# A routed two-layer network behind a sliding filter: a smaller first chunk, and three banks for the second product

## The chip, the cores and the metric

The kernel runs on one core of one Trainium2 chip. The metric is the device time of one execution in microseconds (us); lower is better. The engines are called as the profile calls them: PE (TensorE) multiplies matrices, DVE (VectorE) and ACT (ScalarE) work on elements, POOL (GpSimd) here mostly issues indirect DMAs (DMAs whose rows are picked by a list of indices), SP (SyncE) issues the plain ones.

## The reference

`x` is 8 x 3584 x 192 in float32. It is filtered along the sequence with 7 softmaxed taps for each of 8 heads of 24 columns; then each of the 28672 rows goes to one of 8 experts, the one with the largest logit, and through that expert's two layers:

```python
w = softmax(weight, axis=-1)                                 # 8 heads, 7 taps
out = np.einsum('hk,bskhg->bshg', w, windows_of(x_padded))   # causal filter
x = out.reshape(28672, 192)
logits = x @ w_gate + modality_bias[modality_id]             # 8 experts
e_idx, gate_w = argmax(logits), softmax(logits)[argmax]
for e in range(8):
    h = np.maximum(x[e_idx == e] @ w1[e], 0)                 # 192 -> 1024
    out[e_idx == e] = gate_w * (h @ w2[e])                   # 1024 -> 192
```

## The kernel before

**Routing by groups.** The rows are cut in 256 tiles of 112; four tiles are a quad, and `QUADS_OF_GROUP` makes 19 groups g0 to g18 of 1, 1, 2, 2, 2 and then 14 times 4 quads. A group is loaded (`x` or `xr`), filtered with one step for each head (`convolve`, PE tile `cv`, copied to `y` by ACT or DVE), turned and multiplied with the gate's weights (`turn`, `part_turned`, `gate`, `logits`: tiles `turned`, `gx`, `gt`, `lt`, `lg`), given its experts (`choose`) and its places among the rows of these (`place`: PE tile `rp`, then `idx`). At last one indirect DMA of POOL for each tile writes its 112 rows to the place in DRAM (`send`, tensor `routed_rows`, line 212); one such DMA is called a scatter here. There are four buffers `y`: a group of 4 quads takes two, and a filter step can only write one when its earlier scatters have landed. The first `WHOLE_X` groups are filtered with one product in full float32; for the later ones DVE and ACT split x into a high and a low part (`xh`, `xl`) and PE makes three faster products. `WHOLE_Y` does the same for the gate's product (`gx` are the split parts).

**The network by slots and passes.** The groups are bundled in chunks (`GROUPS_OF_CHUNK`), each with a fixed number of slots (`SLOTS_OF_CHUNK`), each of a fixed number of passes (`PASSES_OF_SLOT`) of 256 rows. A slot serves one expert with rows that are there: a small table (`table`, DVE, about 25 operations on one partition) picks expert and first row; SP reads it and loads the slot's weights (`raw`) and rows (`rows`, `ends`). ACT and DVE split the weights in two parts (`w1b`, `w2b`, line 100 and 101), PE turns the rows of a pass (`tp`), ACT and DVE split them (`sxh`, `sxl`, `sxs`), and the pass then has four steps (`fp` 0 to 3): ten matmuls of the first layer into `hps` (line 695), `hh` by ACT, `hl` by DVE, and, two steps later (`LAG`), eight matmuls of the second layer into `po` (lines 713 and 717). After the last one `put` makes `lowp` (ACT) and `o` (DVE) for both halves, and POOL writes them to the output with two indirect DMAs (line 732), the puts. Rows that fill no slot wait for a later chunk; the last chunk has slots of one pass, of which 8 always run.

**The order.** `start(0)` emits all of the first chunk's groups, the loads of slot 0, and then `AHEAD` more parts of the routing; this is called the head here. Then `run` emits step after step. Between steps it emits parts of the routing as fast as `due` says: `marks` lists the step by which the groups of a chunk must be routed, `LEAD` steps before the chunk begins. Step numbers count from 0 at the first `hps`; the first chunk has 32 steps, and 456 steps run in all. `TURN` is the step of a pass after which the next pass is turned. ACT keeps the order as written; on the other engines a scheduler may move instructions. PSUM has 8 banks: 2 for `hps`, 2 for `po`, 4 for everything else (`ps_t`: `tp`, `cv`, `gt`, `rp`).

Of the kernel before, what the change touches and what calls it, by code (L numbers as in the profile page):

```python
# [9 lines left out]
F32 = mybir.dt.float32  # L10
# [6 lines left out]
PSUM = bass.MemoryType.PSUM  # L17

P = 128
MB = 112  # L20
HALO = 16
QUADS_OF_GROUP = (1, 1, 2, 2, 2) + (4,) * 14
WHOLE_X = 10
WHOLE_Y = 5
HEAD_BANKS = dict(turn=1, logit=2, place=2)
ORDERED = {mybir.EngineType.Activation}
WARM = 50
# [1 line left out]
WAIT = 3  # L29
OUTS = 4  # L30
PIN = 18
AHEAD = 26
T = 256
GROUPS_OF_CHUNK = (5, 2, 2, 2, 2, 2, 2, 2, 0, 0)
SLOTS_OF_CHUNK = (4, 3, 3, 4, 3, 4, 3, 3, 3)
PASSES_OF_SLOT = (2, 4, 4, 4, 4, 4, 4, 4, 2, 1)
LEAD = 11
TURN = 1
LAG = 2
SURE = 8  # L40

# [2 lines left out]
def conv_then_routed_ffn(ctx, tc, x, weight, modality, w_gate, mod_bias, w1, w2, out):  # L44
# [30 lines left out]
    sp = ctx.enter_context(tc.tile_pool(name="sp", bufs=4))  # L75
    hp = ctx.enter_context(tc.tile_pool(name="hp", bufs=4))
    ps_g1 = ctx.enter_context(tc.tile_pool(name="ps_g1", bufs=2, space=PSUM))
    ps_g2 = ctx.enter_context(tc.tile_pool(name="ps_g2", bufs=2, space=PSUM))
    ps_t = ctx.enter_context(tc.tile_pool(name="ps_t", bufs=4, space=PSUM))

    halves = slice(0, DB), slice(DB, P)
    turns = {}
# [1 line left out]
    def ring(pool, n, shape, dtype, name, tag=None):  # L84

        tag = tag or name
        k = turns[tag] = turns.get(tag, -1) + 1
        return pool.tile(shape, dtype, name=name, tag=f"{tag}_{k % n}", bufs=1)
# [94 lines left out]
    def make_modality():  # L183
        both = const.tile([MB, 2, E], F32, name="both")
        nc.scalar.dma_start(out=both.rearrange("p m e -> p (m e)"),
                            in_=mod_bias.rearrange("m e -> (m e)").partition_broadcast(MB))
        step = const.tile([MB, E], F32, name="step")
        nc.vector.tensor_tensor(out=step, in0=both[:, 1, :], in1=both[:, 0, :], op=ALU.subtract)
        rows = N // MB
        ids = raw2[1].rearrange("p c d -> p (c d)")[:, 0:2 * MB * rows // P].bitcast(I32).rearrange("p (q s) -> p q s", s=2 * MB)  # L190
        nc.scalar.dma_start(out=ids, in_=modality.bitcast(I32).rearrange("(q p s) -> p q s", p=P, s=2 * MB))
        low = raw2[1].rearrange("p c d -> p (c d)")[:, 2 * MB * rows // P:3 * MB * rows // P].rearrange("p (q s) -> p q s", s=MB)
        nc.vector.tensor_copy(out=low, in_=ids.rearrange("p q (s two) -> p q s two", two=2)[:, :, ::-1, 0])
        mt_ps = ring(ps_t, 4, [MB, rows], F32, "mt_ps", "t")
        for q in range(rows // P):
            nc.tensor.transpose(out=mt_ps[:, q * P:(q + 1) * P], in_=low[:, q, :], identity=ident)
        mt = const.tile([MB, NB, NSB], F32, name="mt")
        nc.vector.tensor_copy(out=mt.rearrange("p b s -> p (b s)"), in_=mt_ps)
        return both[:, 0, :], step, mt
# [24 lines left out]
    class Group:  # L224
# [13 lines left out]
        def bank(self, use, *args):  # L238

            if self.chunk > 0 or use not in HEAD_BANKS:  # L240
                return ring(ps_t, 4, *args, "t")
            if HEAD_BANKS[use] == 1:
                return ring(ps_g1, 2, *args, "hps")
            return ring(ps_g2, 2, *args, "po")

        def load(self, q):

# [18 lines left out]
        def convolve(self, h):  # L266
            if h == 0:
                self.ys = [routed_y() for _ in range(self.blocks)]
            cv = ring(ps_t, 4, [MB, self.tiles, G], F32, "cv", "t")
            hs = slice(h * G, (h + 1) * G)  # L270
            if self.whole_x:
                terms = ((band, self.x[:, 0:self.tiles, :]),)
            else:
                terms = (band_hi, self.xh), (band_hi, self.xl), (band_lo, self.xh)
            for n, (wt, xt) in enumerate(terms):
                nc.tensor.matmul(cv, wt[:, h, :], xt[:, :, hs], start=n == 0, stop=n == len(terms) - 1)  # L276
            ys = slice(2 + h * G, 2 + (h + 1) * G)
            for i, y in enumerate(self.ys):
                src = cv[:, i * self.nb:(i + 1) * self.nb, :]
                if h % 3 < 2:  # L280
                    nc.scalar.copy(out=y[0:MB, 0:self.nb, ys], in_=src)  # L281
                else:
                    nc.vector.tensor_copy(out=y[0:MB, 0:self.nb, ys], in_=src)
# [165 lines left out]
    def all_groups():  # L449

        cur, ends = Group(0, 0), iter(())
        for q in range(cur.quads):
            cur.load(q)
            cur.part(q)
        for g in range(NG):
            after = Group(g + 1, chunk_of[g + 1]) if g + 1 < NG else None
            done, tiles = 0, 4 * QUADS_OF_GROUP[g - 1]
            for i, _ in enumerate(body(cur, after)):
                yield
                if g < FIRST:  # L460
                    if 1 <= i < H:
                        next(ends, None)
                        if i == H - 1:
                            for _ in ends:
                                pass
                else:
                    while done * (parts_of(g) - 4) < (tiles + 1) * i:
                        next(ends, None)
                        done += 1
            for _ in ends:  # L470
                pass
            ends = finish(cur, 4 if g < FIRST else 1)
            if g + 1 in (FIRST, NG):
                for _ in range(WAIT):
                    yield
                for _ in ends:
                    yield
            cur = after
# [129 lines left out]
    class Slot:  # L608
# [55 lines left out]
        def turn(self, k):  # L664
            lot, k0 = divmod(k, LOT)
            rows = self.rows[lot][:, k0 * NJ:(k0 + 1) * NJ, :]
            tp = ring(ps_t, 4, [P, NJ + 1, P], F32, "tp", "t")
            for j in range(NJ):
                nc.tensor.transpose(out=tp[:, j, :], in_=rows[:, j, 2:2 + P], identity=ident)  # L669
            nc.tensor.transpose(out=tp[:, NJ, :], in_=self.ends[lot][:, k0].rearrange("p j d -> p (j d)"), identity=ident)  # L670
            xh = ring(sp, 2, [P, NJ, P], F32R, "sxh")
            xl = ring(sp, 2, [P, NJ, P], F32R, "sxl")
            xs = ring(sp, 2, [P, NJ, P], F32R, "sxs")
            pieces = [(xh, xl, tp[:, 0:NJ, :])]
            pieces += [(xs[halves[j], j, :], xs[halves[1 - j], j, :], tp[halves[j], NJ, :]) for j in range(NJ)]
            for hi, _, raw in pieces:
                nc.scalar.copy(out=hi, in_=raw)  # L677
            for hi, lo, raw in pieces:
                turned = nc.vector.tensor_tensor(out=lo, in0=raw, in1=f(hi), op=ALU.subtract).ins  # L679
            tag = ring(sp, 8, [P, NJ, 2], F32, "tag")  # L680
            with tc.issue_after(turned):
                nc.vector.tensor_copy(out=tag, in_=rows[:, :, 0:2])
            self.h["x", k] = [z.rearrange("p j s -> p (j s)") for z in (xh, xl, xs)]
            self.h["tag", k] = tag
            state["vector"] = turned
# [16 lines left out]
        def second(self, k, fp):  # L702
            wb = w2b[self.i % 2]
            hh, hl = self.h.pop((k, fp))
            if fp == 0:
                self.po = [ring(ps_g2, 2, [P, 2 * D], F32, "po") for _ in range(NJ)]
            for u in range(2):
                c = 2 * fp + u
                for j, po in enumerate(self.po):
                    js = slice(j * P, (j + 1) * P)  # L710

                    def by_hi():
                        nc.tensor.matmul(po, hh[:, u, js], wb[:, c, :], start=c == 0, stop=c == NF - 1,  # L713
                                         skip_group_check=True)

                    def by_lo():
                        nc.tensor.matmul(po[:, 0:D], hl[:, u, js], wb[:, c, 0:D], start=False, stop=False,  # L717
                                         skip_group_check=True)

                    for product in (by_lo, by_hi) if c == NF - 1 else (by_hi, by_lo):  # L720
                        product()
            if fp == NF // 2 - 1:
                self.put(self.h.pop(("tag", k)))
# [54 lines left out]
    for c in range(1, last):  # L778
        steps += plan[c - 1][1] * steps_of(c - 1)
        g = sum(GROUPS_OF_CHUNK[:c + 1])  # L780
        if not GROUPS_OF_CHUNK[c]:
            break
        marks.append((steps - LEAD, head + sum(parts_of(i) for i in range(FIRST, min(g + 1, NG)))
                      + (WAIT + 2 + 4 * QUADS_OF_GROUP[-1] if g == NG else 0)))

    def due(step):
        for (s0, p0), (s1, p1) in zip(marks, marks[1:]):
# [137 lines left out]
```

## Time and profile before

| | us |
|---|---|
| runs of the kernel before: median (lowest to highest of 3) | 1295.89 (1295.55 to 1296.23) |
| the profiled execution, and its span | 1294.9, 1293.2 |
| PE busy in the span | 1247.0 |
| DVE, ACT, POOL busy in the span | 982.2, 701.5, 523.2 |
| mean granted clock of PE | 0.985 of full speed |

The page gives busy times of one profiled execution, the one line of 40 slices for each engine, and the groups of instructions. A busy PE in it is not PE at its peak, since matmuls overlap; the price of a stretch of PE work is read from the starts of its instructions. Numbers like "75.63" are microseconds from the start of the span.

### The profile page before, as it was taken

The page shows a single profiled execution, that of the slowest core. Times are in us where ns is not written, and L with a number is a line of the kernel's source. Part 1 is how long each engine was busy: PE and PEld are TensorE (multiplying, and loading weights), DVE is VectorE, ACT ScalarE, POOL GpSimd, SP SyncE. Part 2 cuts the span into 40 slices and gives each one's busy share as a digit, 9 for nine tenths or more (in the row PEclk, how much of TensorE's full clock was granted, in tenths as well). Part 3 has the DMA queues.
Part 4 walks back from the last instruction along what each step waited for, and adds up shares of the span by engine and source line. Part 5 has one row for each costly group of instructions (what it writes and reads, how often), then busy time and mean ns, then how long its engine had stood idle before and what let it go on. Part 6 is the DMA issues. An engine that isn't in the chain of part 4 may idle for free.

```text
span 1293.2 us, 27020 instructions
## 1 busy us (share of the span) xinstructions
PE 1247.0 (96%) x9448; PEld 1219.8 (94%) x9448; DVE 982.2 (76%) x2431; ACT 701.5 (54%) x1644; POOL 523.2 (40%) x574
## 2 busy tenths in 40 slices
PE   8559999999999999999999999999999999999997
PEld 7348899999999999999999999999999999999996
DVE  6569977887888677877888777877776666577895
ACT  2236664565656556555555555555554454455784
POOL 5736762626262622625354442614426122122121
PEclk9779999999999999999999999999999999999999
DMA  6576462523443224413254334413314123683230
GB/s 177 158 207 185 122 183 55 144 79 107 118 140 85 74 79 122 142 47 94 62 147 135 103 96 117 133 31 104 96 52 130 32 77 107 159 195 97 87 100 17
DMA packets 158679, 142.10 MB, mean 110 GB/s; under 512 B 43715, under 2 KB 145212, under 8 KB 158533
## 3 DMA queue, kind: packets, MB, share of 16 engines
q1 hardware_dynamic: 132916, 94.93, 27.7%
q0 software_dynamic: 23232, 44.30, 10.8%
q8 instruction: 76, 1.25, 0.4%
q10 hardware_dynamic: 2384, 1.06, 0.3%
q14 instruction: 71, 0.57, 0.1%
HBM read 118.16 MB, written 51.82 MB: 131 GB/s over the span
## 4 chain that ended last, share of the span: by engine, by line
PE 80%; issue 9%; DVE 4%; POOL 4%; DMA 2%; ACT 1%; ACTq 0%; POOLq 0%; SPq 0%; DVEq 0%
PE hps L695 35%; PE po L713 23%; PE po L717 11%; PE cv L276 5%; PE gt L320 3%; POOL routed_rows L212 2%; PE tp L669 2%; POOL out_dram L732 2%; PE tp L670 1%; DVE hl L699 1%; DMA routed_rows<-y,idx 1%; DVE w1b L101 0%; DMA out_dram<-o,tag 0%; DVE turned L300 0%; DVE gx L101 0%
## 5 line engine op out<-in xcount | busy, mean ns | idle before, releaser
L713 PE MATMUL po<-w2b,hh 128*128 128x384 f32 x1824 | 554.7, 355 | 2.9 <-DVE o L731 2.9
L698 ACT ACTIVATE hh<-hps 128x512 fp32r<-128x512 f32 x456 | 272.8, 598 | 420.1 <-PE hps L695 416.4
L695 PE MATMUL hps<-sxh,w1b 128*128 128x256 f32 x1824 | 490.0, 291 | 0.4 <-ACT sxh L677 0.4
L732 POOL DMA_INDIRECT out_dram<-o,tag x228 | 237.8, 1043 | 576.4 <-DVE o L731 514.2
L699 DVE SCALAR_TENSOR_TENSOR hl<-hps,hh 128x512 fp32r<-128x512 f32 x456 | 312.8, 687 | 195.5 <-ACT hh L698 190.4
L717 PE MATMUL po<-w2b,hl 128*128 128x192 f32 x1824 | 441.0, 252 | 0.0
L695 PE MATMUL hps<-sxs,w1b 128*128 128x256 f32 x1824 | 361.7, 280 | 0.0
L695 PEld LDWEIGHTS hps<-sxh,w1b 128*128 128x128 f32 x1824 | 344.0, 189 | 3.1 <-ACT sxh L677 0.6
L713 PEld LDWEIGHTS po<-w2b,hh 128*128 128x128 f32 x1824 | 343.1, 188 | 3.7 <-DVE o L731 3.5
L717 PEld LDWEIGHTS po<-w2b,hl 128*128 128x128 f32 x1824 | 345.4, 190 | 0.0
L212 POOL DMA_INDIRECT routed_rows<-y,idx x256 | 253.7, 991 | 150.0 <-issue 97.3
L695 PEld LDWEIGHTS hps<-sxs,w1b 128*128 128x128 f32 x1824 | 278.9, 189 | 0.1
L695 PE MATMUL hps<-sxl,w1b 128*128 128x256 f32 x912 | 255.9, 281 | 4.1 <-DVE sxl L679 4.1
L695 PEld LDWEIGHTS hps<-sxl,w1b 128*128 128x128 f32 x912 | 173.0, 190 | 6.3 <-DVE sxl L679 4.3
L101 DVE TENSOR_TENSOR w1b<-raw,w1b 128x512 fp32r<-128x512 f32 x152 | 102.5, 685 | 14.0 <-ACT w1b L100 11.9
L729 ACT ACTIVATE lowp<-po,tag 128x192 f32<-128x192 f32 x228 | 83.4, 417 | 31.8 <-PE po L713 31.8
L281 ACT COPY y<-cv 112x192 f32<-112x192 f32 (+1 forms) x198 | 53.7, 317 | 86.5 <-PE cv L276 65.5
L101 DVE TENSOR_TENSOR w2b<-raw,w2b 128x384 fp32r<-128x384 f32 x152 | 82.6, 553 | 16.2 <-ACT w2b L100 16.2
L100 ACT CAST w1b<-raw 128x512 fp32r<-128x512 f32 x152 | 92.3, 620 | 0.2 <-DMA raw<-in_moe_w_dram 0.2
L731 DVE SCALAR_TENSOR_TENSOR o<-po,tag,lowp 128x192 f32<-128x192 f32 x228 | 84.8, 412 | 5.9 <-ACT lowp L729 2.3
L100 ACT CAST w2b<-raw 128x384 fp32r<-128x384 f32 x152 | 75.9, 512 | 0.0
L679 DVE TENSOR_TENSOR sxs<-tp,sxs 64x128 fp32r<-64x128 f32 x228 | 65.8, 289 | 3.1
(136 smaller groups left out, 1089.0 us busy)
## 6 DMA issues: line engine op xcount, KB each, us to landing
raw<-in_moe_w_dram SPq DMA_DIRECT2D x38, 768.0 KB
raw<-in_moe_w_dram SPq DMA_DIRECT2D x38, 512.0 KB
raw<-in_moe_w_dram SPq DMA_DIRECT2D x76, 256.0 KB
xr<-in_x_dram SPq DMA_DIRECT2D x36, 384.0 KB
rows<-routed_rows SPq DMA_DIRECT2D x53, 260.0 KB
x<-in_x_dram SPq DMA_DIRECT2D x26, 384.0 KB
ends<-routed_rows SPq DMA_DIRECT2D x53, 128.0 KB
routed_rows<-filler SPq DMA_DIRECT2D x8, 776.0 KB
```

The costliest lines, as they stand in the source:

```text
L100: nc.scalar.copy(out=hi, in_=raw)
L101: return nc.vector.tensor_tensor(out=lo, in0=raw, in1=f(hi), op=ALU.subtract).ins
L212: state["scatter"] = nc.gpsimd.indirect_dma_start(out=scr, out_offset=bass.IndirectOffsetOnAxis(ap=idx, axis=0), in_=src, in_offset=None,).ins
L679: turned = nc.vector.tensor_tensor(out=lo, in0=raw, in1=f(hi), op=ALU.subtract).ins
L695: nc.tensor.matmul(hps[:, u, :], wa[:, c, fs], mv[z], start=n == 0, stop=n == len(terms) - 1)
L698: nc.scalar.activation(out=hh, in_=hps, func=AF.Relu)
L699: nc.vector.scalar_tensor_tensor(out=hl, in0=hps, scalar=0.0, in1=f(hh), op0=ALU.max, op1=ALU.subtract)
L713: nc.tensor.matmul(po, hh[:, u, js], wb[:, c, :], start=c == 0, stop=c == NF - 1, skip_group_check=True)
L717: nc.tensor.matmul(po[:, 0:D], hl[:, u, js], wb[:, c, 0:D], start=False, stop=False, skip_group_check=True)
L729: nc.scalar.activation(out=lowp, in_=po[:, D:2 * D], func=AF.Copy, scale=gate)
L731: nc.vector.scalar_tensor_tensor(out=o, in0=po[:, 0:D], scalar=gate, in1=lowp, op0=ALU.mult, op1=ALU.add)
L732: st = nc.gpsimd.indirect_dma_start(out=out, out_offset=bass.IndirectOffsetOnAxis(ap=tag.bitcast(I32)[:, j, 1:2], axis=0), in_=o, in_offse ...
```

## The change

The first chunk is made of the first four groups (6 quads, 24 tiles) instead of five (8 quads, 32 tiles), with three slots of 512 rows instead of four; the second chunk has two slots of 1024 rows instead of three, and takes g4 and g5; the last group, g18, goes to the ninth chunk, whose slots have 1024 rows instead of 512. Slots and passes that always run: before 38 slots and 114 passes, now 36 slots and 114 passes. Seven groups instead of ten are filtered in one product, and four instead of five gated so. `AHEAD` falls from 26 to 19 parts, which are those of g4. Up to g6 (`QUICK`) the scatters of a group are emitted in a bunch, and the mark of the second chunk lies 8 steps ahead of it instead of 11. The next pass is turned after step 0 of a pass instead of step 1. `po` has three banks instead of two, and `ps_t` three instead of four.

```diff
-WHOLE_X = 10
-WHOLE_Y = 5
+WHOLE_X = 7
+WHOLE_Y = 4
...
-AHEAD = 26
+AHEAD = 19
 T = 256
-GROUPS_OF_CHUNK = (5, 2, 2, 2, 2, 2, 2, 2, 0, 0)
-SLOTS_OF_CHUNK = (4, 3, 3, 4, 3, 4, 3, 3, 3)
-PASSES_OF_SLOT = (2, 4, 4, 4, 4, 4, 4, 4, 2, 1)
+GROUPS_OF_CHUNK = (4, 2, 2, 2, 2, 2, 2, 2, 1, 0)
+SLOTS_OF_CHUNK = (3, 2, 3, 4, 3, 4, 3, 3, 3)
+PASSES_OF_SLOT = (2, 4, 4, 4, 4, 4, 4, 4, 4, 1)
+QUICK = 6
 LEAD = 11
-TURN = 1
+TURN = 0
...
-    ps_g2 = ctx.enter_context(tc.tile_pool(name="ps_g2", bufs=2, space=PSUM))
-    ps_t = ctx.enter_context(tc.tile_pool(name="ps_t", bufs=4, space=PSUM))
+    ps_g2 = ctx.enter_context(tc.tile_pool(name="ps_g2", bufs=3, space=PSUM))
+    ps_t = ctx.enter_context(tc.tile_pool(name="ps_t", bufs=3, space=PSUM))
...
-                if g < FIRST:
+                if g <= QUICK:
...
-            ends = finish(cur, 4 if g < FIRST else 1)
+            ends = finish(cur, 4 if g < QUICK else 1)
...
-        marks.append((steps - LEAD, head + sum(parts_of(i) for i in range(FIRST, min(g + 1, NG)))
-                      + (WAIT + 2 + 4 * QUADS_OF_GROUP[-1] if g == NG else 0)))
+        marks.append((steps - (LEAD if g > QUICK else 8), head + sum(parts_of(i) for i in range(FIRST, min(g + 1, NG)))
+                      + (WAIT + 2 + 4 * QUADS_OF_GROUP[-1] if g == NG else 0) - (parts_of(g) - H if g <= QUICK else 0)))
```

All uses of the two rings follow (`ring(ps_t, 3, ...)`, `ring(ps_g2, 3, ...)`). The new line shifts the line numbers behind it by one.

Three places show what moves. The first is PE at the end of the head, up to the first turn of rows and the first `hps`. Before:

```order
L276 MATMUL cv<-x,band 112x384 x3
L320 MATMUL gt<-gx,wg_parts 128x256 x13
L276 MATMUL cv<-x,band 112x384 x2
L320 MATMUL gt<-gx,wg_parts 128x256 x11
L669 MATMUL tp<-ident,rows 128x128 x4
L670 MATMUL tp<-ident,ends 128x128 x2
L695 MATMUL hps<-sxh,w1b_89 128x256 x2
```

and now:

```order
L321 MATMUL gt<-gx,wg_parts 128x256 x12
L277 MATMUL cv<-x,band 112x384
L371 LDWEIGHTS tri
L371 MATMUL rp<-oh,tri 112x64
L372 LDWEIGHTS ones
L372 MATMUL rp<-oh,ones 112x64
L277 MATMUL cv<-x,band 112x384
L670 MATMUL tp<-ident,rows 128x128 x2
L671 MATMUL tp<-ident,ends 128x128
L696 MATMUL hps<-sxh,w1b_89 128x256 x2
```

The gate of g5 (24 products of 256 columns) and nine of the twelve filter products of 384 columns that stood ahead of the first `hps` now stand behind it; those of g4 (`rp` of 64 columns) stay ahead of it, and one pass is turned there instead of two.

The second is POOL, from the scatters of g4 (`y_217`) on: `y_218` and `y_219` hold g5, `out_dram` are the puts. Before:

```order
L212 DMA routed_rows<-y_217,idx 238592x194 x8
L360 IOTA y_218 112x8
L360 IOTA y_219 112x8
L290 TENSOR_TENSOR bt<-mt,step 112x128
L293 TENSOR_TENSOR bt<-bt,both 112x128
L212 DMA routed_rows<-y_218,idx 238592x194 x8
L212 DMA routed_rows<-y_219,idx 238592x194 x8
L360 IOTA y_220 112x8
L360 IOTA y_217 112x8
L732 DMA out_dram<-o,tag 28672x192 x2
```

and now:

```order
L213 DMA routed_rows<-y_217,idx 238592x194 x8
L361 IOTA y_218 112x8
L361 IOTA y_219 112x8
L733 DMA out_dram<-o,tag 28672x192 x4
L291 TENSOR_TENSOR bt<-mt,step 112x128
L294 TENSOR_TENSOR bt<-bt,both 112x128
L733 DMA out_dram<-o,tag 28672x192 x2
L213 DMA routed_rows<-y_218,idx 238592x194 x8
L213 DMA routed_rows<-y_219,idx 238592x194 x8
L361 IOTA y_220 112x8
```

POOL's order up to the scatters of g4 is the same; g5's sixteen scatters now stand behind the puts of three passes.

The third is PE at step 20 of the changed kernel, where the rows of the second chunk's first pass are turned; before, that turn stands behind step 29:

```order
L714 MATMUL po<-w2b_91,hh 128x384
L718 MATMUL po<-w2b_91,hl 128x192
L714 MATMUL po<-w2b_91,hh 128x384
L718 MATMUL po<-w2b_91,hl 128x192
L321 MATMUL gt<-gx,wg_parts 128x256
L670 MATMUL tp<-ident,rows 128x128 x2
L321 MATMUL gt<-gx,wg_parts 128x256 x11
L671 MATMUL tp<-ident,ends 128x128
L696 MATMUL hps<-sxh,w1b_89 128x256
```

The last group of the second chunk is placed (`rp`) behind step 13 there, seven steps ahead of this turn; before, it was placed behind step 11, eighteen steps ahead of its turn.

More of the change, by code (lines that the diff above doesn't have):

```diff
@@ L193, in make_modality @@
         nc.vector.tensor_copy(out=low, in_=ids.rearrange("p q (s two) -> p q s two", two=2)[:, :, ::-1, 0])
-        mt_ps = ring(ps_t, 4, [MB, rows], F32, "mt_ps", "t")
+        mt_ps = ring(ps_t, 3, [MB, rows], F32, "mt_ps", "t")
         for q in range(rows // P):
@@ L240, in bank @@
             if self.chunk > 0 or use not in HEAD_BANKS:
-                return ring(ps_t, 4, *args, "t")
+                return ring(ps_t, 3, *args, "t")
             if HEAD_BANKS[use] == 1:
                 return ring(ps_g1, 2, *args, "hps")
-            return ring(ps_g2, 2, *args, "po")
+            return ring(ps_g2, 3, *args, "po")
         def load(self, q):
@@ L268, in convolve @@
                 self.ys = [routed_y() for _ in range(self.blocks)]
-            cv = ring(ps_t, 4, [MB, self.tiles, G], F32, "cv", "t")
+            cv = ring(ps_t, 3, [MB, self.tiles, G], F32, "cv", "t")
             hs = slice(h * G, (h + 1) * G)
@@ L666, in turn @@
             rows = self.rows[lot][:, k0 * NJ:(k0 + 1) * NJ, :]
-            tp = ring(ps_t, 4, [P, NJ + 1, P], F32, "tp", "t")
+            tp = ring(ps_t, 3, [P, NJ + 1, P], F32, "tp", "t")
             for j in range(NJ):
@@ L705, in second @@
             if fp == 0:
-                self.po = [ring(ps_g2, 2, [P, 2 * D], F32, "po") for _ in range(NJ)]
+                self.po = [ring(ps_g2, 3, [P, 2 * D], F32, "po") for _ in range(NJ)]
             for u in range(2):
```

## The prediction

> **What bounds the kernel now.** I read the slices of the page first, then busy times by stretch, then the timeline of the stretch that is not full.
>
> ```profile
> span 1293.2 us, 27020 instructions
> PE   8559999999999999999999999999999999999997
> POOL 5736762626262622625354442614426122122121
> PEclk9779999999999999999999999999999999999999
> ```
>
> A slice is 32.3 us. PE is full from the fourth slice on, so up to about 90 us something else sets the pace, and from there on a gain needs less PE work or fewer early stalls. POOL is busiest in the second slice.
>
> ```profile
> 40.00:60.00 20.00, 10.79 (x35) 5.73 (x33) 9.25 (x43) 4.32 (x14) 15.65 (x18) 0.73 0.43 128
> 60.00:82.00 22.00, 9.63 (x36) 7.09 (x36) 9.15 (x39) 5.92 (x12) 9.46 (x16) 0.55 0.51 138
> 82.00:88.00 6.00, 1.94 (x10) 1.70 (x10) 5.84 (x20) 0.72 (x3) 2.63 (x1) 0.88 1.03 322
> 88.00:120.00 32.00, 30.13 (x214) 28.39 (x214) 30.36 (x69) 21.30 (x51) 21.37 (x23) 0.97 0.72 193
> 88.00:151.00 63.00, 58.62 (x411) 53.79 (x411) 58.89 (x151) 40.31 (x96) 42.23 (x41) 0.98 0.52 148
> 151.00:233.00 82.00, 80.50 (x594) 76.36 (x593) 63.79 (x169) 44.68 (x110) 38.53 (x44) 1.00 0.46 129
> ```
>
> The columns after the length are PE, weight loads, DVE, ACT, POOL, then the granted clock. From 40 to 60 only POOL is busy (15.65 of 20). From 88 to 151 DVE is as full as PE (58.89 and 58.62 of 63), and PE idles 4.4 us; later DVE has air, and PE idles 1.5 us in 82.
>
> How the first slot starts, POOL, then SP, PE and DVE:
>
> ```profile
> 58.26 1.81 POOL L212 DMA_INDIRECT routed_rows<-y,idx  x1 [0.30 <-issue]
> 61.45 0.97 POOL L212 DMA_INDIRECT routed_rows<-y,idx  x1 [0.30 <-issue]
> 70.19 1.03 POOL L212 DMA_INDIRECT routed_rows<-y,idx  x1 [0.30 <-issue]
> ```
>
> ```profile
> 70.75 0.37 SPq L620 DMA_DIRECT2D raw<-in_moe_w_dram  x1
> 75.63 0.39 SPq L641 DMA_DIRECT2D rows<-routed_rows  x1
> ```
>
> ```profile
> 75.90 2.90 PE L276 MATMUL cv<-x,band 128*112 128x384 f32 x4 [6.90 <-ACT y L281]
> 78.02 2.56 PE L320 MATMUL gt<-gx,wg_parts 128*128 128x256 f32 x11
> 80.42 0.60 PE L669 MATMUL tp<-ident,rows 128*128 128x128 f32 x4
> 81.59 0.50 PE L695 MATMUL hps<-sxh,w1b 128*128 128x256 f32 x2 [0.35 <-ACT sxh L677]
> 86.16 0.38 PE L695 MATMUL hps<-sxl,w1b 128*128 128x256 f32 x1 [4.07 <-DVE sxl L679]
> ```
>
> ```profile
> 81.83 2.49 DVE L101 TENSOR_TENSOR w1b<-raw,w1b 128x512 fp32r<-128x512 f32 x4
> ```
>
> 58.26 is the last scatter of g3, 61.45 to 70.19 are the eight of g4, one in 1.25 us. The rows of slot 0 are asked for 5.44 us after the last one, and step 0 begins at 81.59; PE then waits 4.07 us, since DVE splits the weights only now. The head is a chain of POOL's scatters.
>
> **The change, part by part.** The sum is made against the profiled execution, 1294.9 us; the median of the runs is 1295.9, 1.0 above it.
>
> *The first slot needs 24 scatters instead of 32.* POOL's order up to g4 is unchanged, so the last one needed is that of 58.26, 11.93 us earlier, and the rows are asked for at 63.7. The traffic after the request says when they land:
>
> ```profile
> GB/s 131 262 164 360 197 262 197 98 131 0 0 0 0 46 67 25 46 125 183 300 333 337 337 309 295 289 264 184 107 39 37 37 25 61 98 197 276 240 301 344
> ```
>
> This is 75 to 80 us in slices of 0.125: the rows are the hump that ends at about 78.7, 3.1 us after the request. Before, PE was at that time in `cv` and `gt` of later groups; now only g4's and three filter products of g5 stand ahead of the turn, and I take them as done. So the turn is at 66.8, and step 0, as before 1.17 us later, at 68.0: **-13.6**. Ends: -11.9 (nothing of the tail shortens), and -16.5, if the scatters land as fast as the quickest (2.5 instead of 5.44):
>
> ```profile
> DMA to landing us min/median/max: 2.5/4.3/6.2
> ```
>
> The Trainium skill (DMA: Bandwidth & Descriptors, section Anatomy of one DMA) gives about 2.0 us plus bytes over 436 GB/s for such a DMA, an estimate of 2.2 us for 112 rows of 776 bytes; by it the sum would be 3.2 us lower. The measured 5.44 includes more, so the trace does not bear it out here.
>
> *The wait of 4.07 us at step 0 goes.* The weights' table no longer stands behind g5's work on DVE, so the splits of `w1b` fit into the wait for rows: -4.1. Against it, PE idles before step 0 and its clock is low (0.55 from 60 to 82, 0.88 from 82 to 88); that cost fell into the stall and now falls on matmuls: 0.12 x 6 = 0.7 lost, 1.2 with the steps before it; ends 0 and 3. **-2.9**. The Trainium skill (TensorE: Matmul & The Clock Gate, Part 1) says that PE runs at half speed after an idle window of about 3.4 us, until it was busy for as long; the granted clock agrees. By that rule the loss would be 1.7 instead of 1.2, and the sum 0.5 higher.
>
> *PE work that moves or changes.* Prices from the starts of instructions:
>
> ```profile
> 93.93 1.30 PE cv L276 x4
> 195.70 1.44 PE gt L320 x12
> ```
>
> ```profile
> 290.13 0.34 PE L276 MATMUL cv<-xh,band_hi 128*112 128x384 f32 x1
> 290.66 0.34 PE L276 MATMUL cv<-xh,band_hi 128*112 128x384 f32 x1
> ```
>
> A filter product in full float32 is two instructions, 0.65 us; a split one is three, 0.53; a gate product 0.12. Counted in PE's order behind step 0: 28 of the first become 13 (-9.8), 72 of the second 96 (+12.7), 312 gates 336 (+2.9): **+5.9**, certain within 0.5; before, three fifths of it lay in the idle head.
>
> *DVE in the first 48 steps.* By DVE's order there stand, against before, 4 more `turned`, 4 more `gx`, 12 `xl` where none was, 4 `y` copies (0.35 each), one more choose and place (some 16 operations, the longest 0.42, taken as 4.5 together), and 4 `w2b` splits fewer (-2.2):
>
> ```profile
> L300 DVE STREAM_TRANSPOSE turned<-y 128x768 f32<-128x768 f32 x64 | 61.1, 965 | 6.0 <-ACT y L281 5.5
> L101 DVE TENSOR_TENSOR gx<-turned,gx 128x768 fp32r<-128x768 f32 x56 | 53.4, 953 | 8.1 <-ACT gx L100 7.6
> L101 DVE TENSOR_TENSOR xl<-xr,xh 128x768 fp32r<-128x768 f32 x36 | 34.3, 953 | 2.7 <-ACT xh L100 2.6
> L101 DVE TENSOR_TENSOR w2b<-raw,w2b 128x384 fp32r<-128x384 f32 x152 | 82.6, 553 | 16.2 <-ACT w2b L100 16.2
> L283 DVE COPY y<-cv 112x192 f32<-112x192 f32 x62 | 20.3, 345 | 14.4 <-PE cv L276 8.6 <-DMA routed_rows<-y,idx 5.7
> L376 DVE TENSOR_TENSOR_SCAN base<-keep,ad 112x128 f32<-112x128 f32 x14 | 5.9, 424 | 0.4
> ```
>
> 3.9 + 3.8 + 11.4 + 1.4 + 4.5 - 2.2 = 22.8. From 88 to 233, where step 48 begins, DVE was busy 58.89 + 63.79 = 122.7; now 145.5. It was never fuller than 30.36 of 32, 95%; at that it needs 153.3 us. PE alone needs the 145 less 5.9 of idle, plus about 5 of the work above, 144. So PE would lose 9.3 instead of 5.9: **+3.4**; ends -2 (tighter interleaving) and +7 (DVE at 93%). ACT, at 64%, is no bound.
>
> *The second chunk's first rows.* Step 20 turns rows that need the scatters of g5, placed behind step 13. Seven steps of
>
> ```profile
> 1046.18 0.37 PE L695 MATMUL hps<-sxh,w1b 128*128 128x256 f32 x1
> 1055.80 0.36 PE L695 MATMUL hps<-sxh,w1b 128*128 128x256 f32 x1
> ```
>
> 9.62 / 4 = 2.405 us, with six filter products and a gate, are 22.2, with DVE's share of delay 23.5. The rows need the time from place to the first scatter, 15 more scatters, and landing and load. For g6 of the kernel before:
>
> ```profile
> 123.12 0.22 PE L371 MATMUL rp<-oh,ones 112*112 112x128 bf16 x1
> 126.64 0.94 POOL L212 DMA_INDIRECT routed_rows<-y,idx  x1 [4.95 <-ACT hh L698]
> 148.63 0.94 POOL L212 DMA_INDIRECT routed_rows<-y,idx  x1 [0.30 <-issue]
> 155.83 0.37 SPq L641 DMA_DIRECT2D rows<-routed_rows  x1
> ```
>
> 3.5 + 15 x 1.25 + 5.44 + 3.1 = 30.8, a wait of about 7 us at step 20. While PE waits, DVE works off what it is behind, which is most of the term above; I count **+3**. Ends 0 and +12.3: g6's own pace, 32.7 + 3.1 = 35.8, less 23.5.
>
> *Costed at nothing.* The weights of the second chunk are first split behind step 16, soon after their table: ACT may wait, but PE has two steps in hand (0 to +3). `ps_t` with three banks: 0 to +4, covered by copies that follow soon; if DVE is late, PE waits with it. `po` with three banks takes away at most
>
> ```profile
> PE po L713 <- DVE o L731: 2.9, 3, 1.5
> ```
>
> 2.9 us, part of the idle counted above. Two slots fewer spare ACT and DVE 16 weight splits, late ones under a full PE. The tail has the same 114 passes.
>
> Sum: -13.6 - 2.9 + 5.9 + 3.4 + 3.0 = -4.2: 1290.7 for the profiled execution, **1291.7** for the median.
>
> **Rivals.**
> *All of it hides.* DVE keeps up and the rows come in time: without the last two terms -10.6, 1285.3. For it: ACT and POOL have air; against: DVE at 95% was never exceeded.
> *The rows of the second chunk come late.* POOL sets step 20: at g6's pace the wait is 12.3 and nothing of it is absorbed, -4.2 - 3 + 12.3 = +5.1, 1301.0. It decides from a counted wait of 7.2 on. For it: slack shrinks from eighteen steps to seven, and g5's scatters stand behind six puts; against: no puts stand between them, as eight did for g6.
> *The head does not shorten.* The weights were asked for at 70.75, only 5 us ahead of the rows. If their table stays that late, the first two terms are lost, +5.9 + 3.4 = +9.3, 1305. Against: the table reads g3's end, and nothing of g5 stands ahead of it now.
>
> **How the numbers follow.** Differences under 0.2% (2.6 us) can't be told from none. Forecast 0.48 (0.38 faster, 0.10 same); all hidden 0.20 (faster); rows late 0.22 (0.06 same, 0.16 slower); head unchanged 0.05 (slower); the bank costs at their ends 0.05 (0.01 faster, 0.01 same, 0.03 slower). Faster 0.59, same 0.17, slower 0.24. The range goes from below all hidden to late rows, 1282 to 1302; the forecast's own is 1287 to 1296.
>
> **What would show it.** First `hps` near 68 with no wait of 4 us behind it; the `tp` of step 20 waiting some 7 us for a load of rows; DVE at 95% up to step 48; step 48 at about 228 (before 233); the rest as before. Wrong it would be if step 48 begins after 233, or if waits for rows or weights return at a later chunk's start.

## Result: 35 us slower, and the profile after

| | before | changed |
|---|---|---|
| median (lowest to highest), us | 1296.06 (1295.55 to 1298.11) | 1331.14 (1330.05 to 1331.92) |
| profiled execution, span, us | 1294.9, 1293.2 | 1330.4, 1328.4 |
| PE, DVE busy in the span, us | 1247.0, 982.2 | 1260.7, 974.4 |

The ratio is 1.0267, with a 95% interval of 1.0249 to 1.0285. Forecast were 1291.7 and a range of 1282 to 1302: the sign and the range are wrong. Eight of the experiments below (f, g and h) ran on two other chips, called the slow chips here: the kernel before took 1530 us on both, and the mean granted clock was 0.91 (the last section shows where PE stood still). They are given as ratios to the kernel before on the same chip, and what they say of size was measured again on the first chip, at full clock.

The slices of the changed kernel's page, to lay beside those of before:

```profile
span 1328.4 us, 27025 instructions
PE   8579698799999999999999999999999999999997
POOL 3734467354535262353535253352626122222222
PEclk8789899899999999999999999999999999999998
```

A slice is 33.2 us now. PE, which was full from the fourth slice on, now has holes in the fifth, seventh and eighth, with a lower clock in the fifth and the eighth. Busy time by stretch (columns: length, PE, weight loads, DVE, ACT, POOL, clock, DMA), up to step 0 and from there to step 48, first of before, then of the changed kernel:

```profile
0.00:81.59 81.59, 55.77 (x292) 41.51 (x292) 45.78 (x202) 21.78 (x65) 46.07 (x73) 0.81 0.59 166
81.59:233.16 151.57, 141.63 (x1013) 132.17 (x1014) 129.06 (x339) 85.70 (x208) 83.87 (x87) 0.99 0.51 144
```

```profile
0.00:72.61 72.61, 48.34 (x236) 35.68 (x236) 40.98 (x187) 17.17 (x50) 43.09 (x67) 0.76 0.61 168
72.61:256.21 183.60, 157.97 (x1074) 148.06 (x1075) 145.30 (x378) 97.51 (x229) 87.05 (x91) 0.93 0.48 138
```

Step 0 begins at 72.61 instead of 81.59 (-9.0), but the 48 steps behind it take 183.6 us instead of 151.6 (+32.0). From step 48 to the end of the span it is 1072.2 instead of 1060.0 (+12.2). The three make +35.2: 23.0 of it lie ahead of step 48 and 12.2 behind it. What PE waited for, over the whole span:

```profile
PE po L714 <- DVE o L732: 15.9, 18, 6.3
PE cv L277 <- ACT xh L101: 11.4, 3, 7.8
PE tp L670 <- DMA rows<-routed_rows: 8.3, 1, 8.3
```

The last is the wait for the first rows, ahead of step 0. The other two are new; before, `po` waited 2.9 us for `o`, and `xh` was never waited for. Three places show them. The first is step 18, on SP, ACT and PE:

```profile
128.22 0.35 SPq L621 DMA_DIRECT2D raw<-in_moe_w_dram  x1
134.98 0.62 ACT L101 CAST w1b<-raw 128x512 fp32r<-128x512 f32 x1 [5.64 <-DMA raw<-in_moe_w_dram]
136.82 0.73 ACT L730 ACTIVATE lowp<-po,tag 128x192 f32<-128x192 f32 x2
139.51 0.69 PE L714 MATMUL po<-w2b,hh 128*128 128x384 f32 x1 [6.27 <-DVE o L732]
```

The second chunk's weights are asked for at 128.2. ACT, which keeps its order, stands 5.64 us at their cast; `lowp` of the pass that has just ended is queued behind the cast, `o` needs `lowp`, and PE needs `o` to have the bank again. The second place is step 45, on SP, ACT and PE:

```profile
238.57 0.37 SPq L642 DMA_DIRECT2D rows<-routed_rows  x1
240.99 6.28 SPq L255 DMA_DIRECT2D xr<-in_x_dram  x4
245.05 0.83 ACT L101 CAST xh<-xr 128x768 fp32r<-128x768 f32 x1 [8.89 <-DMA xr<-in_x_dram]
245.93 0.66 PE L277 MATMUL cv<-xh,band_hi 128*112 128x384 f32 x1 [7.75 <-ACT xh L101]
```

A group's fourth quad of x is loaded only when one of three buffers `xr` is free, and on SP that load (the first of the four) stands behind the loads of rows, which wait for the scatters of the group before. PE idles 7.75 us. The third place is the passes from there on: 13 waits of `po`, up to 1 us each, 6.8 us in all behind 256 us, on top of smaller gaps.

### The profile page after: what moved, and what is told of

The parts are those of the page before. It is cut to its first block, busy times and chain, and to the rows that moved or that the text cites. A ratio compares the mean times of both kernels' runs of the same rounds, so it can differ in the third digit from the quotient of the medians.

```text
span 1328.4 us, 27025 instructions
## 1 busy us (share of the span) xinstructions
PE 1260.7 (95%) x9460; PEld 1233.0 (93%) x9460; DVE 974.4 (73%) x2428; ACT 710.1 (53%) x1642; POOL 546.8 (41%) x574
## 4 chain that ended last, share of the span: by engine, by line
PE 77%; DVE 8%; issue 7%; ACT 2%; DMA 2%; POOL 2%; SPq 0%; POOLq 0%; DVEq 0%; ACTq 0%
PE hps L696 33%; PE po L714 22%; PE po L718 10%; PE cv L277 5%; PE gt L321 4%; DVE hl L700 2%; PE tp L670 2%; POOL out_dram L733 1%; PE hps L116 1%; DVE turned L301 1%; PE tp L671 1%; DVE gx L102 1%; DVE sxs L680 1%; DVE o L732 1%; DMA xr<-in_x_dram 1%
## 5 line engine op out<-in xcount | busy, mean ns | idle before, releaser
L714 PE MATMUL po<-w2b,hh 128*128 128x384 f32 x1824 | 560.5, 357 | 16.4 <-DVE o L732 15.9
L733 POOL DMA_INDIRECT out_dram<-o,tag x228 | 261.1, 1145 | 589.6 <-DVE o L732 509.4
L714 PEld LDWEIGHTS po<-w2b,hh 128*128 128x128 f32 x1824 | 344.2, 189 | 21.7 <-DVE o L732 21.3
L102 DVE TENSOR_TENSOR w1b<-raw,w1b 128x512 fp32r<-128x512 f32 x144 | 97.5, 687 | 17.0 <-ACT w1b L101 17.0
L101 ACT CAST w1b<-raw 128x512 fp32r<-128x512 f32 x144 | 87.4, 620 | 11.7 <-DMA raw<-in_moe_w_dram 11.7
L680 DVE TENSOR_TENSOR sxl<-tp,sxh 128x256 fp32r<-128x256 f32 x114 | 48.0, 421 | 62.0 <-ACT sxs L678 61.7
L102 DVE TENSOR_TENSOR w2b<-raw,w2b 128x384 fp32r<-128x384 f32 x144 | 77.6, 550 | 15.1 <-ACT w2b L101 15.1
L678 ACT CAST sxh<-tp 128x256 fp32r<-128x256 f32 x114 | 42.8, 375 | 68.0 <-PE tp L671 65.6
```

What stands on the lines that cost most here:

```text
L102: return nc.vector.tensor_tensor(out=lo, in0=raw, in1=f(hi), op=ALU.subtract).ins
L733: st = nc.gpsimd.indirect_dma_start(out=out, out_offset=bass.IndirectOffsetOnAxis(ap=tag.bitcast(I32)[:, j, 1:2], axis=0), in_=o, in_offse ...
```

## Experiments

Most are single edits, back from the changed kernel or into the kernel before; k1, k3 and m1 (and f1, f3, g1, g3, h1) join several. The times of one call belong together; across calls the ratios to the kernel before are compared.

**The banks.** e1 is the changed kernel with `ps_t` of four banks and `po` of two; e2 the kernel before with three and three.

```diff
-    ps_g2 ... bufs=3, ps_t ... bufs=3      (e1: back to 2 and 4)
+    ps_g2 ... bufs=2, ps_t ... bufs=4      (e2: the opposite, in the kernel before)
```

> The changed kernel with the banks as before: ps_t four, po two; all else as changed. Theory A (the fourth bank of ps_t is what the head and the later passes miss): PE no longer idles at 15 to 18 us and its clock does not fall there, the first scatter is issued near 26 us instead of 31.7, the first hps begins near 67 instead of 72.6, and the 12 us that the stretch behind step 48 is longer than before go too: 1331 - 5 - 11 = 1315. Theory B (only the head misses the bank; the late waits of po come from the earlier turn): 1326, and the stretch behind step 48 stays at 1072 us. Theory C (the banks do nothing): 1331 within 3.

> The kernel before with three banks for ps_t and three for po, nothing else changed. Theory A: the head starts some 5 us later, and po waits for DVE in passes behind step 48, 1296 + 5 + 11 = 1312. Theory B: 1296 + 5 = 1301, nothing behind step 48. Theory C: 1296 within 3.

Measured: e1 1333.9, ratio 1.0297 (1.0271 to 1.0323), nothing gained. Its two halves move against each other: step 0 begins at 69.5 and step 48 at 250.4, 5.8 us earlier than in the changed kernel, but from step 48 to the end it takes 1080.6 us instead of 1072.2. There `po` is waited for longer than the 6.8 us of the changed kernel:

```profile
PE po L714 <- DVE o L732: 11.2, 18, 1.2
```

So the third bank of `po` helps the changed kernel behind step 48. e2 1291.7, ratio 0.9965 (0.9952 to 0.9977): the three banks alone make the kernel before *faster*. Theories A and B are wrong on the time of both runs, though right that the head is later with three banks; theory C has e1's time, but not what happened in it. In e2 the filter's products on PE at the very start:

```profile
17.00 0.49 PE L276 MATMUL cv<-x,band 128*112 128x96 f32 x2 [1.65 <-DVE y L283]
17.88 4.29 PE L276 MATMUL cv<-x,band 128*112 128x96 f32 x20 [0.40 <-issue]
```

With a fourth bank (e1) the same products run at full clock and stand ahead of 19.5 us; here twenty take 4.29 us at a granted clock of 0.50, the first scatter goes out at 31.7 instead of 26.0, and step 0 begins at 86.88 instead of 81.59. The bank is only part of that: in k0, also with three banks, the clock did not fall there, and the first scatter went out at 28.1. And then it costs nothing:

```profile
86.88:232.44 145.56, 141.41 (x1018) 131.82 (x1017) 125.09 (x334) 85.55 (x208) 80.89 (x86) 0.99 0.53 149
```

The stretch up to step 48 is 6.0 us shorter than before, PE's idle in it falls from 9.9 to 4.2, and step 48 comes at 232.4 (before 233.2). A first step that is 5.3 us later is made up by step 48; a likely reason is that the same routing has to be done by then, whenever step 0 begins. It is no rule: k0, the changed kernel profiled again, has step 0 at 69.1 instead of 72.6 and step 48 at 250.0 instead of 256.2, so nothing is given back there. The profiled pair shows 1.3 of the 4.4 us of the medians; where the rest lies is not shown.

**The filter in three products for g7 to g9.** e3 goes back to ten groups in one product; k4 keeps seven, but gives `xr` a fourth buffer and issues the fourth load with the other three. k0 is the changed kernel again, for comparison with k4, k1 and k3.

```diff
-WHOLE_X = 7
+WHOLE_X = 10                                                   (e3)
...
-ring(xp, 3, [P, 4, D], F32, "xr")
+ring(xp, 4, [P, 4, D], F32, "xr")                              (k4, f4, g4)
-            for q in range(min(3, after.quads)):
+            for q in range(min(3 if after.whole_x else 4, after.quads)):
-                if q == 0 and after.quads > 3:
-                    after.load(3)
```

> The changed kernel with ten groups filtered in one product instead of seven (g7 to g9 lose their split of x). Theory A (the split of x for g7 to g9 makes ACT wait for loads of xr that stand late in SP's row, and PE behind it): the 11.4 us of waits of cv for xh go, and with them most of the lower clock behind them (about 4), against 96 split products of 0.53 replaced by 96 of 0.65 beside less work on DVE: about 1331 - 11 - 4 + 4 = 1320. Theory B (PE would have waited for something else at these places): 1331 within 4.

> The changed kernel as it is, run again on the chip of the next three, so that they can be compared with it. At full clock 1331 within 3; on a chip with a granted clock of 0.91, where PE is slower and covers waits, all theories expect a smaller loss, 1.5 to 2.5% over the kernel before.

> The changed kernel with four xr buffers and the fourth load issued with the other three. Theory A (that load stood behind the rows on SP): no wait of cv for xh over 2 us is left, and against k0 it is 10 to 16 us faster at full clock, 4 to 10 on a slow chip. Theory B (the split is late by itself): waits for xh or xl stay, within 4 us of k0.

Measured: e3 1312.8, ratio 1.0126 (1.0100 to 1.0153), 18.4 us below the changed kernel, as much as theory A and 7 us more; against k0 the ratio falls by 1.07%, 14 us. The gain lies ahead of step 48, which comes at 236.8 instead of 256.2. k0 1327.1, 1.0233 (1.0216 to 1.0250); k4 1319.1, 1.0167 (1.0131 to 1.0203), 8.0 us below k0. On the slow chips the kernel of k4 stood at 1.0113 and 1.0132; the changed kernel itself was not run there. The waits of PE in k4:

```profile
PE po L712 <- DVE o L730: 15.6, 18, 6.0
PE cv L277 <- DVE xl L102: 4.0, 4, 1.2
PE cv L277 <- ACT xh L101: 0.8, 1, 0.8
```

The wait for `xh` falls from 10.8 (k0) to 0.8, so it was the fourth load; the edit gives it a buffer and an earlier place on SP at once, and which of the two counts is not told apart. Some of it comes back as waits for `xl` (1.4 in k0, 4.0 here), and `po` waits as before; so k4 gains 8 us where A gave 10 to 16. The other 6 to 10 us of e3 would then be the split's own work on ACT and DVE; that was not tried by itself.

**The turn.** e4 is the changed kernel with `TURN = 1`, m2 the kernel before with `TURN = 0`; f2 is the kernel of m2 on a slow chip.

> The changed kernel with the next pass turned after step 1 of a pass, as before, instead of step 0. Theory A (the early turn puts the casts of sxh and sxs and the differences sxl ahead of lowp and o, so the first product into po waits): the waits of po for DVE behind step 48 go, the stretch behind step 48 shrinks from 1072 to about 1061, 1320. Theory B (the late waits come from the banks): the stretch stays within 2 us, 1331 within 3.

> The kernel before with the next pass turned after step 0 instead of step 1, nothing else. Theory A (the early turn alone makes po wait for o, behind step 48 above all): waits of po for DVE of 15 us or more, 1296 + 10 to 18 = 1306 to 1314. Theory B (only in the changed kernel): 1296 within 3.

Measured: e4 1321.3, ratio 1.0189 (1.0172 to 1.0206). m2 1321.8, ratio 1.0210 (1.0187 to 1.0232): this one number, alone, costs the kernel before, with its two banks of `po`, 25.9 us, more than theory A gave it. f2 was 1.0094 (1.0063 to 1.0125). Behind step 48, before and m2, same columns as above:

```profile
233.16:1281.00 1047.84, 1047.07 (x8129) 1043.87 (x8128) 806.20 (x1889) 593.31 (x1369) 391.30 (x414) 1.00 0.37 102
```

```profile
234.70:1306.00 1071.30, 1057.19 (x8130) 1048.41 (x8129) 794.96 (x1892) 597.80 (x1369) 413.80 (x414) 1.00 0.35 99
```

The same matmuls take 23.5 us more, in a stretch that the prediction held for full and safe; 13.3 us of it are idle time of PE (14.1 against 0.8), the rest counts as busy. The end of a pass (step 401) on ACT and DVE, before:

```profile
1151.31 0.69 DVE L699 SCALAR_TENSOR_TENSOR hl<-hps,hh 128x512 fp32r<-128x512 f32 x1 [1.03 <-ACT hh L698]
1151.54 0.73 ACT L729 ACTIVATE lowp<-po,tag 128x192 f32<-128x192 f32 x2 [0.26 <-PE po L713]
1152.00 0.74 DVE L731 SCALAR_TENSOR_TENSOR o<-po,tag,lowp 128x192 f32<-128x192 f32 x2
1153.51 0.42 DVE L679 TENSOR_TENSOR sxl<-tp,sxh 128x256 fp32r<-128x256 f32 x1
```

and in m2, with PE:

```profile
1172.48 0.42 DVE L679 TENSOR_TENSOR sxl<-tp,sxh 128x256 fp32r<-128x256 f32 x1 [0.36 <-ACT sxs L677]
1173.65 0.73 ACT L729 ACTIVATE lowp<-po,tag 128x192 f32<-128x192 f32 x2 [0.26 <-PE po L713]
1173.78 0.69 DVE L699 SCALAR_TENSOR_TENSOR hl<-hps,hh 128x512 fp32r<-128x512 f32 x1
1175.16 0.14 DVE L531 COPY total<-cum 1x1 f32<-1x1 f32 x1
1175.25 0.42 DVE L731 SCALAR_TENSOR_TENSOR o<-po,tag,lowp 128x192 f32<-128x192 f32 x1
1175.72 0.44 PE L713 MATMUL po<-w2b,hh 128*128 128x384 f32 x1 [0.66 <-DVE before L534]
```

Before, `o` begins 0.46 us behind the start of `lowp`, and the next pass's `sxl` and `sxs` come after it. Turned a step earlier, these stand ahead of `lowp` and `o`; `hl` slides behind them, five small operations of the table get in ahead of `o`, and `o` begins 1.60 us behind the start of `lowp`. PE has one step of first-layer work to cover it, and waits. This pass is one of the slow ones: of the 101 passes behind step 48, `o` begins more than 1.2 us behind `lowp` in 23 (before in none), and in the median 0.67 us behind it (before 0.45). That is theory A of e4, shown by m2 for two banks of `po`.

In the changed kernel the delay of `o` is the same (median 0.67 us, 23 passes over 1.2), but the third bank takes the first half of the next pass, and only the second half waits: 6.8 us behind step 48, where e1 with two banks waits 11.2 and takes 8.5 us longer. So the 25.9 us are not the price of the turn in the changed kernel.

That price is e4's 9.9 us, or 5.7 by the profiled pair and by the ratio to k0. Of e4's own stretch behind step 48 only 3.5 us went (1068.6 against 1072.2), although its waits of `po` fell from 15.9 to 3.3 over the whole span, and none is left behind step 48. What took their place shows in k1, below.

**What is left: the smaller first chunk.** k1 is the changed kernel with `WHOLE_X = 10` and `TURN = 1`; k3 the kernel before with only the new tables of groups, slots and passes, `AHEAD = 19`, `WHOLE_Y = 4` and the three banks; m1 is k1 with the second chunk's mark 12 steps ahead instead of 8. On the slow chips the same kernels are f1 and g1, f3 and g3, h1.

> The changed kernel with ten groups in one product and the turn after step 1. Theory A (two separate causes): against k0 28 us faster at full clock (1303). Theory B (they share a stall): 23 us faster (1308).

> The kernel before with the new tables, 19 parts ahead and three banks each, but scatters, marks and turn as before. Theory A (the smaller first chunk is a gain by itself): 1285 at full clock, 7 us below the banks alone. Theory B (what the head saves is given back behind step 0 and at the second chunk's start): 1295 to 1303.

> The kernel of k1_whole_and_turn (1305.4, ratio 1.0062 to before) with the mark of the second chunk 12 steps ahead instead of 8. Theory A (the second chunk's start is late): the stall of 3.2 us at step 18 goes and some of the low clock and of the idle between steps 16 and 48 with it, 3 to 6 us faster, 1300 to 1302. Theory B (only the place of the waiting moves): 1305 within 2. In both some 8 us stay that k1 has behind step 48, where its steps take 58.1 us for 24 instead of 57.65.

Measured, with the ratio to the kernel before:

| | us | ratio | step 0 | step 48 | 48 to end |
|---|---|---|---|---|---|
| before | 1296.1 | 1 | 81.6 | 233.2 | 1060.0 |
| e2, banks alone | 1291.7 | 0.9965 | 86.9 | 232.4 | 1059.5 |
| k3 | 1309.5 | 1.0089 (1.0072 to 1.0107) | 72.3 | 239.0 | 1069.3 |
| k1 | 1305.4 | 1.0062 (1.0045 to 1.0078) | 72.7 | 235.6 | 1069.3 |
| m1 | 1307.0 | 1.0096 (1.0073 to 1.0120) | 69.5 | 233.3 | 1069.4 |
| changed | 1331.1 | 1.0267 | 72.6 | 256.2 | 1072.2 |

k1 is 21.7 us below k0, near theory B. In ratios to before that is -1.71%, and e3 and e4 make -1.07 and -0.44% against k0, but -1.41 and -0.78% against the first measurement of the changed kernel; so whether the two edits add is not settled. k3 is slower than the banks alone by 1.24%, 16 us, and slower than before: its theory A is wrong, and the new tables (with `AHEAD` and `WHOLE_Y`, which were not tried apart from them) are no gain even without the other edits. Step 0 comes 14.6 us earlier than in e2, step 48 6.6 us later. The bunch of scatters and the later mark that goes with it (k1 against k3) help by 4 us. An earlier mark (m1) gains nothing: from step 0 to step 48 it takes 163.8 us, k1 162.9. Theory B of that run holds at full clock; on a slow chip the earlier mark had been better (h1 0.9994, g1 1.0035), which stays unexplained.

The last column holds a surprise. Against the kernel before, k1, k3, m1 and e4 lose 9 us behind step 48, where PE waits for almost nothing. Of k1:

```profile
235.62:1292.00 1056.38, 1056.08 (x8128) 1052.89 (x8127) 798.77 (x1862) 588.74 (x1362) 394.88 (x416) 1.00 0.36 103
```

8128 matmuls in 1056.1 us of busy PE, against 8129 in 1047.1 before, at a clock of 1.00 in both. Steps 400 to 424, which hold no routing, take 58.09 us instead of 57.67, in every kernel with the new tables and the turn after step 1, and 57.60 in the changed kernel itself, with the turn after step 0. Nearly all of it is in the first layer's matmuls. The new tables give the first chunk six passes instead of eight, which shifts all rings of buffers against each other; whether this is the reason was not tried, and the cause stays open. It would hide most of what `TURN = 1` gives back in e4.

On the slow chips:

> The changed kernel with both edits that helped alone: ten groups filtered in one product, and the turn after step 1. Theory A (two separate causes, which add): 1331.1 - 18.4 - 9.9 = 1303, with no wait for xh left, po waiting under 4 us in all. Theory B (they share the stall at step 18): about 1308. In both the rest against before, 7 to 12 us, is the smaller first chunk with its bunched scatters.

> The kernel before with the next pass turned after step 0 instead of step 1, nothing else. Theory A (the early turn by itself puts its casts ahead of lowp and o, whatever the banks): po waits for o in many passes, 1296 + 8 to 12 = 1306. Theory B (it costs only in the changed kernel, where DVE is later): 1296 within 3.

> The kernel before with the new tables of groups, slots and passes, the 19 parts ahead, four groups gated in one product and the three banks each; but ten groups filtered in one product, the turn after step 1, scatters and marks as before (no bunch up to g6, all marks 11 steps ahead). Theory A (the smaller first chunk is a gain once the other edits are gone): the head's 9 to 11 us stay won in part, about 1285 against 1291.7 of the banks alone. Theory B (the head was not what set the time: the routing that it moves behind step 0 takes DVE and POOL there as long as before, and rows or weights of the second chunk come late): 1295 to 1303, step 48 at or behind 233 us.

> The changed kernel with four buffers for the unsplit x (xr) instead of three, so that the fourth quad's load is issued with the other three and not behind the loads of rows on SP; seven groups filtered in one product as changed. Theory A (the waits of cv for xh, 11.4 us, come from that fourth load, which stands behind rows in SP's order): they go, and the low clock behind them, 1331 - 11 - 4 = 1316. Theory B (the split of x is late by itself, since ACT and DVE are full): waits for xh or xl of 8 us or more stay, 1327 or more.

> The same kernel as f1_whole_and_turn (ten groups in one product, turn after step 1), now wanted at full clock, where waits of PE are not hidden under a slower PE. Theory A (two separate causes): 1331.1 - 18.4 - 9.9 = 1303, step 0 near 71, step 48 near 234, no wait for xh, po waiting under 4 us in all. Theory B (shared stall): 1308.

> The same kernel as f3_chunks_plain (before with the new tables, 19 parts ahead and the three banks, but scatters, marks and turn as before), now wanted at full clock. Theory A (the smaller first chunk is a gain by itself): 1285 against 1291.7 of the banks alone. Theory B (what the head saves is given back behind step 0, where DVE has the same routing to do, and at the second chunk's start): 1295 to 1303; step 0 near 72, step 48 at or behind 233.

> The same kernel as f4_xr_early (changed kernel with four xr buffers, the fourth load issued early), now wanted at full clock. Theory A (the waits for xh come from the fourth load behind the rows on SP): the 11.4 us of waits of cv for xh go and with them about 4 of low clock, 1316. Theory B (split late by itself): 1327 or more.

> The kernel of g1_whole_and_turn with the mark of the second chunk 12 steps ahead of it instead of 8, so that its rows are placed, its table made and its weights asked for some four steps earlier. Theory A (what is left of the loss is the second chunk's late start: weights that land after ACT and PE want them, rows that wait for the bunched scatters): the stall at step 18 and the wait for rows at step 20 shrink, 4 to 8 us faster than g1. Theory B (up to step 48 DVE has more to do than PE, so an earlier mark only moves the waiting forward): within 2 us of g1, or slower.

Measured: f1 1.0021 and g1 1.0035, f3 and g3 1.0026, f4 1.0113 and g4 1.0132, f2 1.0094, h1 0.9994. Read as ratios, f2, f4 and g4 lie nearer their theory A, h1 has its theory A (6.4 us below g1), f3 and g3 their theory B, and f1 and g1 lie below both. All are losses or no difference, and smaller than at full clock. The order of f4 and f2 there, as that of k4 and m2 at full clock, is within the noise. None of the runs at full clock beats the banks alone, which is the best version measured, 0.35% faster than before.

## Why the prediction was wrong, step by step

**A term that was not there: the turn.** The list of costs holds the banks, the weights, the table and the rows, but no line for `TURN = 0`. m2 puts 25.9 us on it in the kernel before; within the changed kernel it is 6 to 10 (e4), since the third bank of `po` covers part of the waits and, with the turn after step 1, the slower steps take their place. The sentence that failed is "The tail has the same 114 passes": the same work, but with another order on DVE. From step 48 to the end it took 12.2 us more.

**The split of x: counted as work, not as a place in a queue.** The 12 `xl` on DVE and the cheaper products on PE were in the sum (-9.8, +12.7, +11.4 of DVE). That the loads of `xr` stand behind the loads of rows on SP, and that the fourth one needs a buffer, was not. It cost 11.4 us of waits: 8.0 us by k4; with the work, 14 (against k0) to 18.4 by e3, the largest single cost found in the changed kernel. Of the 23.0 us that step 48 came late, e3 takes back 19.4.

**"The weights ... PE has two steps in hand (0 to +3)".** The wait was 6.27 us. Two steps were in hand for the weights' own use; but ACT keeps its order, and `lowp` stood behind the cast that waited.

**What stays open.** With both edits taken back (k1) some 8 us are left over the kernel before. Behind step 48 k1 takes 9.3 us more (1069.3 against 1060.0) in matmuls that run slower, and no run shows the reason. The prediction's tail had no term for that either.

**DVE's 22.8 us.** DVE was busy for 145.3 us from step 0 to step 48; forecast were 145.5. So near a hit is partly luck: the forecast started from the stretch behind 88 us, and from step 0 on DVE had been busy for 129.1 before, so it grew by 16.2, not by 22.8. The fullness was wrong: "at that it needs 153.3 us" took 95% from a stretch without long waits, and with PE, ACT and SP waiting for each other it was 145.3 of 183.6, 79%. The +3.4 was a bound for a pipeline that runs, not for one that stalls.

**PE's moved work, +5.9.** Of the right order: busy time times granted clock is 157.97 x 0.93 = 146.9 against 141.63 x 0.99 = 140.2, +6.7. But the low clock around each stall was not in the sum: from step 0 to step 48 PE was busy for 19.0 us at a granted clock of 0.50 (72.6 to 78.4, 136.4 to 143.2, 163.7 to 167.1 and 242.3 to 252.5), half of which, 9.5, is lost, against 1.7 of 3.4 before.

**The head, -13.6 and -2.9.** The second half held: PE no longer stands for `sxl` behind the first `hps`, where it had waited 4.07 us. Of the first, the 24 scatters went as fast as read (31.7 to 64.5), but from a start 5.7 us later. The third bank, costed at "0 to +4, covered", is about 2 of that (28.1 in k0 against 26.0 before), and the low clock goes with the rest. The rows were asked for 3.3 us behind the last scatter instead of 5.44, which gave 2.1 back. Step 0 came at 72.6 instead of 68.0; in k0 at 69.1. What was also not sure is that it is worth its face value: e2 has step 0 5.3 us late and loses nothing, and k3 has it 14.6 us earlier than e2 and step 48 6.6 later.

**Rows at step 20, +3.** The rows were asked for 27.7 us after the place (118.1 to 145.8), 27.7 forecast. They were no longer the last to come, since PE had just stood 6.3 us for the weights.

The prediction's own sign of being wrong, step 48 behind 233, came true at 256.2. Of the rivals none held the size: "rows late" (1301) and "head unchanged" (1305) had the right sign and the wrong place. All of them varied terms that were on the list, and what decided was not on it.

## What to carry to other kernels

Give every changed constant a line of its own in the sum, with the engine's queue on which it moves an operation and what stands behind it there; a one-digit edit cost 6 to 10 us here, and 26 in the kernel before. On a queue that keeps its order, a step's slack is that of the most urgent instruction behind it, not its own. And a first step that begins earlier is worth only what the next stage doesn't give back: look where the two kernels meet again before counting it.

## What the hardware showed

- The same kernel has two heads. In the changed kernel's first profile PE's clock fell to 0.50 from 17 to 27 us, after idles of 1.65 and 0.40 us around two products; in k0, with the same two idles, it did not, and the same twenty products took 2.90 us instead of 4.29:

```profile
17.83 4.29 PE L277 MATMUL cv<-x,band 128*112 128x96 f32 x20 [0.40 <-issue]
```

```profile
17.31 2.90 PE L277 MATMUL cv<-x,band 128*112 128x96 f32 x20 [0.40 <-issue]
```

  The first scatter went out at 31.7 and 28.1. The Trainium skill (TensorE: Matmul & The Clock Gate, Part 1) says that activity is judged in a window that runs free of the kernel, so that its phase differs from run to run; these two traces agree with that. The idle here, 2.05 us in two pieces, is shorter than the idle window of about 3.4 us that the prediction took from the same place, and the clock fell all the same; the measurement decides. In the nine profiles with three banks on the first chip the first scatter is at 31.7 in six, at 29.9 in e3, and near 28 in k0 and m1.
- The slow chips were not evenly slow. In f1 PE had full stretches at a clock of 1.00 and others, 15 to 19 us long, in which little was issued though the trace names nothing that was waited for; here the third of three rows, 10 us each, of the busy times:

```profile
440.00:450.00 10.00, 10.00 (x76) 9.99 (x75) 6.90 (x19) 4.73 (x13) 2.76 (x3) 1.00 0.14 46
450.00:460.00 10.00, 9.11 (x67) 8.69 (x65) 4.00 (x11) 2.73 (x9) 7.56 (x9) 1.00 0.24 70
460.00:470.00 10.00, 3.65 (x13) 2.96 (x13) 0.69 (x1) 0.60 (x1) 7.70 (x11) 0.66 0.23 71
```

  In the five such stretches between 458 and 838 us POOL, issuing scatters, is busy for 53 to 65% of the time; between them it is busy for 28 to 30%, and PE is nearly full. In k1, the same kernel at full clock, PE is busy for 24.00 of 24 us (454 to 478) under such a bunch. So the low mean clock goes with PE standing still during scatters; why it does so on those chips is not known.

- Equal matmuls in equal order, at equal clock, took 0.7% longer in one family of kernels (k1, k3, m1, e4): 58.09 us for steps 400 to 424 in each, against 57.67 before.
